# The third of sixteen units moves from the early kind of work to the later kind

## The chip, the cores and the metric

One core of one Trainium2 chip runs one program. The metric is the device time of one execution in microseconds (us). Its engines work in parallel, each through its own queue in order: PE (TensorE, the matrix engine), DVE (VectorE), ACT (ScalarE), POOL (GpSimd) and SP (SyncE, which here issues every transfer). They wait for each other through semaphores. A matrix product leaves its result in PSUM, of which this kernel uses four tiles ("banks" in the code, b_70 to b_73 in its instructions).

## The reference

Windowed attention, half of the heads with a dense window of 32 and half with a dilated one, and behind it a two-layer feed-forward net on the 4,608 tokens (8 batches of 576), 512 features wide and 2,048 inside:

```python
scores = where(mask, q @ k.T / sqrt(D), -1e9)          # 8 batches, 8 heads, 576 tokens, D = 64
attn   = softmax(scores) @ v
x      = attn, heads side by side                      # 4608 x 512
h      = x @ w_in                                      # 512 x 2048
g      = h * tanh(softplus(h))
out    = g @ w_out                                     # 2048 x 512
```

## The kernel before

**Units.** The work is cut into 16 units of 288 tokens (half a batch each), numbered 0 to 15. A unit's attention has two kinds, 0 (dense) and 1 (dilated). Its x goes through the first layer in eight pieces ff*u*.0 to ff*u*.7, each of two groups of twelve 288-column products (every number is held as two f16 parts, and three products of parts are added), and then through the second layer.

**Two kinds of unit.** Units 0, 1 and 2 are early (constants `FIRST = 3` and `DIRECT = 3`). There the masks are added by PE, the probabilities are turned by PE (L684), the values are multiplied in f32 (L710 with tile `vf`), x is turned by PE (L759), and the second layer is plain: sixteen groups of twelve 288-column products (L991, steps fo). Units 3 to 15 are late (`SEVENS = range(3, 16)`). There the masks are added by DVE, the values are held as two stacked f16 parts in `vh` (L551, L553, and three copies by transfer, L559 and L561), the probabilities are split in two by ACT and DVE and turned by a transfer (L671 to L676), and so is x (L750 to L754). Their second layer takes seven products of half size in place of eight (L952, steps fq: 336 products of 144 columns), with sums of parts of the gate made by DVE (L928) and sums of parts of w_out.

**Between the kinds.** Both weights are loaded as raw 64-bit words and split by ACT and DVE (steps wl, wm, ww, ws, wp) in a memory pool named `early`. Step ol gives that pool back and opens `late`, in which the late units' tiles live (among them the raw values `vn`, the turned probabilities `pT`, and one tile `x16` for both kinds' x). When the last plain second layer no longer reads w_out, step rs rescales it in four parts (L847), and steps su make its sums (L866, L859, L862). The late units' seven products need these sums, and the plain second layer must be over before.

**Order.** Nothing is scheduled by a program at build time: the table ORDER lists some 2,000 steps. A step is a generator, and each mention runs it to its next yield, so the table fixes every engine's queue. "=2" behind a name picks the PSUM tile. va is the value product, tx the turning of x, sp the score products, kw and kh products whose results nobody reads.

The lines that the steps below touch most, in transpose_x:

```python
            x16 = take("x16", x16s)[:nq, :4 * nb * P]
            nc.scalar.copy(hi, xs)
            nc.vector.tensor_tensor(lo, xs, hi, op=ALU.subtract)
            nc.sync.dma_start_transpose(x_span(d, kind).rearrange("k (g q) -> k g q", q=nq), x16)
```

ff1 takes the four 128-row blocks of x in the order kind 0, kind 0, kind 1, kind 1, so its third product already needs both kinds.

Of the kernel before, what the change touches and what calls it, by code (L numbers as in the profile page):

```python
# [41 lines left out]
wl0.0.0 mf wl0.3.0 ww0.3.0 wl0.0.1 ld0 ld0 lv0 mf qp0 ww0.0.0 wm0.0.0 ld0 ld0 ww0.0.1 cs1 ww0.0.0 cs0 kw12 lv0  # L42
wl0.3.1 lv1 wm0.3.0 kh30 kw4 wm0.0.1 ww0.0.0 ww0.3.1 ww0.3.0 kw12 ww0.0.1 ld1 sp0.1=0 sp0.1 ww0.0.1 ws0.0=1 lv0
ww0.3.0 wm0.3.0 sp0.0=2 sp0.0 ww0.3.0 sc0.1 ws0.0 sc0.0 sc0.1 ww0.3.0 lv0 ld1 wm0.3.1 sc0.0 ww0.3.1 qp1 ex0.1 ex0.0
ld1 ww0.3.0 ws0.3=3 tp0.1=1 ws0.3 wp0.0.1 tp0.0=0 wp0.3.0 ww0.3.1 sp1.0=2 xa0 wp0.3.0 tp0.1 ld1 sp1.0 wp0.0.0 sc1.0
sp1.1=3 sp1.1 sc1.0 lv0 sc1.1 kw5 sc1.1 wp0.3.1 wp0.0.0 va0.1=1 pr0 tp0.0 pr0 va0.1 ex1.0 va0.1 ex1.1 wp0.3.1 pr0=0
kw3 tp1.1=2 wl0.1.0 va0.0=3 pr0 wl0.2.1 va0.0 va0.1 va0.1 va0.0 tx0.1=0 ww0.1.0 va0.0 wl0.1.1 va0.0 wm0.1.0 wp0.0.1
lv1 fs0.0 tx0.1 tx0.0=1 wl0.2.0 tx0.0 tx0.1 ww0.1.1 lv2 tp1.0=3 ww0.2.1 tx0.0 tp1.1 wm0.1.1 ww0.1.0 ff0.0=0 wm0.2.1
ff0.0 ld2 tp1.0 ld2 wm0.2.0 lv1 ww0.1.0 ff0.7=1 ww0.2.0 ff0.0 ww0.1.1 ww0.2.1 ws0.1=2 ws0.1 ww0.1.1 ff0.6=3 fs0.3
wp0.1.0 ww0.2.0 ff0.7 ww0.2.0 ff0.6 wp0.1.1 ws0.2=2 qp2 ff0.1=0 wp0.1.1 ws0.2 ff0.6 lv1 ff0.7 wl1.0.0 wp0.1.0 fs0.1  # L50
ww0.2.1 fs0.2 lv1 sp2.0=3 wp0.2.0 sp2.0 wp0.2.1 ff0.1 ff0.3=1 ft ff0.1 wp0.2.0 wm1.0.0 ww1.0.0 ff0.3 fs0.4 ff0.2=2
wp0.2.1 sc2.0 ff0.2 ww1.0.0 ww1.0.0 ff0.2 ff0.3 ff0.4=0 gt0.1=0 ff0.4 ff0.4 va1.0=3 va1.1=2 pr1 va1.0 va1.0 ff0.5=1
gt0.3=1 pr1 wl1.0.1 pr1=0 gt0.3 gt0.0=2 ww1.0.1 ld2 ff0.5 pr1 va1.1 va1.0 wm1.0.1 va1.1 ld2 va1.0 wl1.1.0 va1.1
ff0.5 va1.1 sp2.1=0 ww1.0.1 fs1 tx1.0=3 xa1 tx1.0 tx1.1=1 ws1.0=2 tx1.0 wl1.1.1 tx1.1 ww1.1.0 tx1.1 ws1.0 wm1.1.0
sp2.1 sc2.1 gt0.2=3 ff1.2=3 ff1.5=1 wp1.0.0 lv2 ff1.3=2 ld3 ff1.6=0 gt0.0 ff1.2 ww1.0.1 ww1.1.1 ww1.1.0 ff1.5 ff1.2
wp1.0.0 lv2 ww1.1.0 gt0.1 wm1.1.1 ex2.1 wp1.0.1 ff1.6 wl1.3.1 ff1.0=3 ff1.5 lv2 gt0.2 xa2 ff1.3 ww1.1.1 ff1.0
ws1.1=1 wp1.0.1 ff1.3 ff1.7=2 ff1.0 tp2.1=3 ws1.1 wm1.3.1 lv2 ww1.1.1 wp1.1.0 ff1.7 tp2.1 fo0.0.0=1 pr2 fo0.0.1
ex2.0 tp2.0=3 ff1.6 ff1.4=0 wl1.3.0 ff1.4 ff1.7 wp1.1.1 fo0.0.2 pr2 wp1.1.1 pr2=2 wp1.1.0 tp2.0 ff1.1=3 pr2 fo0.0.3
va2.0=2 ww1.3.1 ff1.4 va2.1=0 va2.1 wl1.2.0 fo0.0.3 wm1.3.0 ww1.3.1 va2.0 va2.0 va2.1 va2.0 va2.1 gt1.1=4 ff1.1
ww1.3.0 wl1.2.1 fo0.1.0 gt1.3=5 va2.1 va2.0 tx2.1=0 ww1.3.0 wm1.2.0 gt1.1 tx2.1 tx2.0=2 ld3 tx2.1 tx2.0 fs2 tx2.0  # L60
ww1.3.1 ff1.1 gt1.2=6 ww1.3.0 fo0.1.1 wm1.2.1 ww1.2.1 ww1.2.1 ld3 ws1.3=0 fo0.1.2 qp3 fo0.1.3 ff2.6=2 ww1.2.0
ww1.2.0 fo0.1.3 ff2.0=3 gt1.2 gt1.0=7 ff2.0 ff2.0 gt1.3 ff2.7=1 ff2.2=3 fo0.0.3 gt1.0 fo0.1.3 ws1.3 ww1.2.0 ws1.2=0
wp1.3.1 ww1.2.1 ff2.2 ws1.2 wp1.3.1 wp1.3.0 ld3 wp1.2.1 ff2.6 wp1.2.0 ff2.6 ff2.7 ff2.4=0 ff2.4 ff2.2 sp3.0=2
wp1.2.0 sp3.1=3 sp3.1 ld4 sp3.0 wp1.2.1 ff2.7 wp1.3.0 ff2.4 mr=1 ol ff2.5=0 mr mr ff2.5 fo0.2.0=1 fo0.2.1 sc3.1 lv3
fo0.2.2 fo0.2.3 ld4 ff2.5 ex3.1 fo1.0.0=3 lv3 sc3.0 ex3.0 fo0.2.3 fo1.0.1 lv3 fo0.3.0 gt2.3=2 fo0.3.1 tp3.0 tp3.0
pr3 lv3 pr3 ld4 pr3=0 gt2.2=0 ff2.1=2 tp3.1 tp3.1 pr3 ff2.1 fo0.3.2 tp3.1 pr3 pr3 ff2.3=0 xa4 tp3.1 ld4 ff2.1
gt2.0=3 lv4 fo1.0.2 qp4 fo1.0.3 gt2.0 tp3.0 lv4 vx3 ff2.3 fo1.0.3 fo0.3.3 gt2.3 ff2.3 sp4.1=2 sp4.0=0 sp4.0 lv4 vx3
fo0.2.3 lv4 fo1.0.3 sc4.0 sp4.1 vx3 gt2.1=1 gt2.1 fo1.1.0 fo1.1.1 fo0.3.3 sc4.1 ex4.0 pr4 tp3.0 ld5 gt2.2 qp5
fo1.1.2 fo2.0.0=0 fo1.1.3 ld5 fo1.1.3 fo2.0.1 fo2.2.0=1 va3.0=2 va3.1=3 va3.0 va3.1 pr4 ld5 va3.0 fo2.2.1 va3.0
va3.1 fo0.3.3 pr4=2 tp4.0 tp4.0 pr4 fo2.2.2 fo1.1.3 va3.1 fo2.0.2 pr4 fo1.2.0=2 pr4 ld5 fo2.2.3 fo2.2.3 fo2.0.3  # L70
tp4.0 lv5 sp5.1=3 lv5 xa3 sp5.1 tx3.0 fo1.2.1 lv5 fo1.2.2 lv5 sc5.1 fo2.0.3 ex4.1 fo2.3.0 fo2.3.1 tp4.1 fo2.1.0
tp4.1 sp5.0=3 tp4.1 tx3.0 sp5.0 fo2.1.1 fo2.1.2 fo2.3.2 ld6 vx4 pr5 sc5.0 ex5.1 tx3.0 vx4 tx3.1 tp4.0 fo2.1.3
fo2.0.3 vx4 fo1.2.3 fo2.1.3 fo2.2.3 fo1.2.3 va4.0=3 tp4.1 va4.0 fo1.2.3 fo2.3.3 fo2.1.3 fo1.3.0 fo1.3.1 fo2.3.3
va4.0 tp5.1 tp5.1 fo1.3.2 fo1.3.3 so tx3.1 fo1.3.3 va4.1=0 pr5 tx3.1 rs rs rs fs4 rs va4.1 su0=3 su0 ff3.5=1 ff3.0=2
tp5.1 su0 ff3.0 va4.0 tp5.1 fs3 va4.1 ex5.0 ld6 rs ff3.4=3 tx4.0 su1=1 su0 tx4.0 su1 tx4.0 fo1.3.3 ff3.4 va4.1 ff3.0
ff3.1=2 ff3.4 ff3.1 tp5.0 tp5.0 su0 tx4.1 su1 tx4.1 su1 ff3.5 ff3.7=0 ff3.5 ld6 su0 ff3.2=3 ff3.1 gq3.0.0=0 su0
# [1004 lines left out]
```

## Time and profile before

| | us |
|---|---|
| median of 3 runs | 849.95 (846.66 to 851.33) |
| the profiled execution, its time | 850.15 |
| its span, first to last instruction | 848.4 |
| PE busy in it | 825.8 |

The span is the part that the trace shows; 1.75 us of the profiled execution lie around it. A row of the trace gives a start, a duration, an engine, the line of the kernel, the operation with its output and inputs, and in brackets the idle time ahead of it and who ended it. PE's rows can hold many matmuls merged, with a small overlap at their ends.

### The profile page before, as it was taken

How to read it: one execution, taken by the hardware profiler on the slowest of the kernel's cores; microseconds unless marked ns; L12 is line 12 of the kernel's file. 1: busy time of each engine (PE TensorE's matmuls, PEld its weight loads, DVE VectorE, ACT ScalarE, POOL GpSimd, SP SyncE). 2: the span in 40 equal slices, each digit the busy share in tenths (PEclk: the TensorE clock that was granted, in tenths of full speed). 3: DMA queues.
4: the chain of work that ended last, by engine and by line, in shares of the span. 5: the costliest groups of instructions: out<-in, count | busy, mean ns of one | idle time of the engine just before them, and what ended most of it. 6: DMA issues, size and time to landing. Idle time of an engine off the chain costs nothing.

```text
span 848.4 us, 29902 instructions
## 1 busy us (share of the span) xinstructions
PE 825.8 (97%) x13706; PEld 712.2 (84%) x13706; DVE 600.9 (71%) x770; ACT 489.3 (58%) x608; POOL 40.4 (5%) x80
## 2 busy tenths in 40 slices
...
DMA packets 157581, 98.18 MB, mean 116 GB/s; under 512 B 92496, under 2 KB 150864, under 8 KB 157456
## 3 DMA queue, kind: packets, MB, share of 16 engines
...
q8 instruction: 107, 1.75, 0.9%
...
## 4 chain that ended last, share of the span: by engine, by line
PE 70%; DVE 10%; DMA 9%; SPq 4%; ACT 4%; issue 3%; DVEq 0%; ACTq 0%
PE b L809 33%; PE b L952 25%; PE b L991 5%; PE b L602 3%; PE b L710 2%; DVE g L866 2%; DMA vn<-in_v 1%; DVE g L922 1%; DMA w<-in_w_in 1%; DMA vh<-vh 1%; DMA x<-x 1%; SPq L513 1%; DMA knd<-in_kdT 1%; DVE hm L928 1%; SPq L676 1%
## 5 line engine op out<-in xcount | busy, mean ns | idle before, releaser
L809 PE MATMUL b<-x,w 128*128 128x288 f16 x3072 | 395.2, 286 | 4.3 <-DMA x<-x 2.3
L809 PEld LDWEIGHTS <-w 128*128 128x128 f16 x3072 | 294.3, 97 | 79.1 <-issue 4.3
L922 DVE SCALAR_TENSOR_TENSOR g<-hm,sg,g 128x1152 f16<-128x1152 f32 (+1 forms) x104 | 129.8, 1263 | 70.0 <-ACT g L920 69.8
L815 ACT ACTIVATE hm<-b,fs 128x576 f32<-128x576 f32 x128 | 92.6, 737 | 135.6 <-PE b L809 116.0
L952 PE MATMUL b<-g,w 128*128 128x144 f16 x2496 | 166.6, 226 | 0.6 <-DVE g L922 0.6
L952 PEld LDWEIGHTS <-w 128*128 128x128 f16 x2496 | 159.2, 98 | 3.3 <-issue 0.7
L920 ACT ACTIVATE g<-hm,sg 128x1152 f16<-128x1152 f32 (+1 forms) x104 | 115.7, 1127 | 46.6 <-PE b L952 30.5
L928 DVE TENSOR_TENSOR hm<-hm 128x576 f32<-128x576 f32 x104 | 80.4, 779 | 3.2 <-ACT hm L815 2.2
L966 ACT ACTIVATE y<-b,fo 128x288 f32<-128x288 f32 x52 | 40.4, 780 | 58.7 <-PE b L952 57.3
L991 PE MATMUL b<-g,w 128*128 128x288 f16 x576 | 73.1, 286 | 0.0
L991 PEld LDWEIGHTS <-w 128*128 128x128 f16 x576 | 55.8, 98 | 14.2
L971 DVE SCALAR_TENSOR_TENSOR y<-b,fo,y 128x144 f32<-128x144 f32 x78 | 33.4, 477 | 47.6 <-PE b L952 23.9
L952 PE MATMUL b<-g,g 128*128 128x144 f16 x936 | 66.0, 226 | 0.0
L952 PE MATMUL b<-g,late_sums 128*128 128x144 f16 x936 | 65.4, 226 | 0.0
L952 PEld LDWEIGHTS <-g 128*128 128x128 f16 x936 | 60.8, 98 | 1.4
L952 PEld LDWEIGHTS <-late_sums 128*128 128x128 f16 x936 | 60.2, 98 | 0.5
L618 DVE SCALAR_TENSOR_TENSOR sb<-b,m_p 96x768 f32<-96x768 f32 (+2 forms) x26 | 24.1, 927 | 23.4 <-PE b L602 20.0
L553 DVE SCALAR_TENSOR_TENSOR vh<-vn,s,vh 128x2688 f16<-128x2688 f32 (+1 forms) x13 | 35.2, 2708 | 6.2 <-ACT vh L551 6.2
L551 ACT ACTIVATE vh<-vn,s 128x2688 f16<-128x2688 f32 (+1 forms) x13 | 29.7, 2288 | 11.4 <-issue 7.4
L489 POOL COPY qp<-qn 128x576 f32<-128x576 f32 x15 | 25.0, 1664 | 203.2 <-DMA qn<-in_qT 145.9
L730 DVE TENSOR_TENSOR xs<-b,rec 128x768 f32<-128x768 f32 (+1 forms) x32 | 30.6, 956 | 2.6
L331 DVE TENSOR_REDUCE m<-vn 128x1 bf16<-128x1024 f32 (+1 forms) x19 | 20.3, 1068 | 15.2 <-DMA vn<-in_v 12.7
(131 smaller groups left out, 735.7 us busy)
## 6 DMA issues: line engine op xcount, KB each, us to landing
...
```

The costliest lines, as they stand in the source:

```text
L551: nc.scalar.activation(hi, src, AF.Identity, scale=s)
L553: nc.vector.scalar_tensor_tensor(lo, src, s, hi, ALU.mult, ALU.subtract)
L730: nc.vector.tensor_tensor(xs.rearrange("p (a t h e) -> p a t h e", a=2, h=2, e=D), avv[:, :, :, 1:AW - 1].rearrange("p a t (h e) -> p a t ...
L809: nc.tensor.matmul(ph[:, h, :HT], w1[j][:, c, wi, k * P:(k + 1) * P], x_of(d, xi, c), start=(n == 0), stop=(n == len(seq) - 1))
L815: nc.scalar.activation(d["m"][p][:, half, k0:k0 + 2], ph[:, :, :HT], AF.Mish, scale=d["fs"][:, j:j + 1])
L920: nc.scalar.activation(hi, src, AF.Identity, scale=sg)
L922: nc.vector.scalar_tensor_tensor(lo, src, sg, hi, ALU.mult, ALU.subtract)
L928: nc.vector.tensor_tensor(a, a, b, op=op)
L952: nc.tensor.matmul(acc[e], left(l, e, p, wi)[:, k * P:(k + 1) * P], right(gi, k), start=(n in opens and p == 0 and q == 0), stop=(last and ...
L966: nc.scalar.activation(into(half, t), by(acc), AF.Identity, scale=fo)
L971: nc.vector.scalar_tensor_tensor(o, by(acc)[:, e], fo, o, ALU.mult, ALU.add)
L991: nc.tensor.matmul(po[:, :HT], w2[:, e, j, wi, k * P:(k + 1) * P], d["g"][j][:, gi, k, :], start=(j == 0 and n == 0), stop=(j == NCH - 1 a ...
```

## The change

Three constants go from 3 to 2, so that unit 2 is a late unit: its values are stacked, its probabilities and its x are turned by transfers, its second layer takes seven half-size products, and only units 0 and 1 have a plain second layer. The scale of the output (`fo`) gets a function of its own, since unit 2's scale can be made only behind rs while its other scales are needed ahead of it. The table ORDER is a new one throughout, the start included: kw and kh steps differ, and the loads come in another order.

```diff
-    FIRST = 3
-    DIRECT = 3
-    SEVENS = range(3, 16)
+    FIRST = 2
+    DIRECT = 2
+    SEVENS = range(2, 16)
...
-        if u >= FIRST:
-            nc.scalar.activation(d["fo"], h_o, AF.Identity, scale=d["f_v"])
+        if u > FIRST:
+            out_scale(u)
+
+    def out_scale(u):
+
+        nc.scalar.activation(U[u]["fo"], h_o, AF.Identity, scale=U[u]["f_v"])
...
-             "ex": exps, ... "fs": ff_scales,
+             "ex": exps, ... "fs": ff_scales, "fp": out_scale,
...
-kh30 kw4 wm0.0.1 ww0.0.0 ww0.3.1 ww0.3.0 kw12 ww0.0.1 ld1 sp0.1=0 sp0.1
+kw12 lv1 ww0.3.0 ww0.3.0 ld0 cs0 cs1 xa1 kh162 mf ww0.3.0 ww0.3.0 sp0.0=0
```

What stands where the plain second layers end and the first late unit's first layer begins, on three engines. (Line numbers of the changed kernel are up to 6 higher.)

PE before: the last rows ahead of ff3. pT_2102 with vh is the value product of unit 4, kind 1; x with w_88 is ff3.

```order
L991 MATMUL b_72<-g_102,w_90 128x288
...
L710 MATMUL b_70<-vh,pT_2102 32x65
L809 LDWEIGHTS w_88
L809 MATMUL b_71<-x,w_88 128x288
```

PE after: the last three plain groups, the value product of unit 2, kind 1 (pT_1760), the scores of unit 4 (knp and knd), and ff2 (x with w_86).

```order
L997 MATMUL b_73<-g_101,w_90 128x288
...
L997 MATMUL b_73<-g_104,w_90 128x288
...
L997 MATMUL b_70<-g_97,w_90 128x288
...
L712 MATMUL b_73<-vh,pT_1760 32x65
L604 MATMUL b_71<-knp,qp 32x64 x24
L604 MATMUL b_72<-knd,qn 32x56 x32
L604 MATMUL b_71<-knp,qp 32x64 x12
L604 MATMUL b_72<-knd,qn 32x56 x16
L815 LDWEIGHTS w_86
L815 MATMUL b_70<-x,w_86 128x288
```

Ahead of ff the plain groups and the values of the unit after next stood on PE; now the values of the very unit that ff takes stand there, with four rows of scores between.

DVE before: xs is a unit's normalised x before turning, x_2104 its split into x16. The rows are of unit 3, whose ff comes next; L847 is the rescaling.

```order
L752 TENSOR_TENSOR x_2104<-xs_2817,x_2104 128x768
L997 TENSOR_SCALAR fo<-h_o,f 128x1
L530 TENSOR_REDUCE m_3087<-vn 128x1
L838 TENSOR_REDUCE const_o<-f_o 128x1
L839 RECIPROCAL const_o<-const_o 128x1
L841 TENSOR_SCALAR const_o<-f_o,const_o 128x4
L842 TENSOR_SCALAR const_o<-const_o,top_92 128x1
L843 COPY h_o<-const_o 128x4
L847 TENSOR_SCALAR w_90<-w_90,const_o 128x4096 x3
```

DVE after: the rows of unit 2. L853 is the rescaling of the last part of w_out, L872 the sums, L555 the split of unit 3's values.

```order
L853 TENSOR_SCALAR w_90<-w_90,const_o 128x4096
L730 RECIPROCAL rec<-den 128x12
L732 TENSOR_TENSOR xs_2609<-b_73,rec 128x768
L754 TENSOR_TENSOR x_1762<-xs_2527,x_1762 96x768
L872 TENSOR_TENSOR g_98<-w_90 128x1024
L872 TENSOR_TENSOR g_98<-g_98,w_90 128x1024
L555 SCALAR_TENSOR_TENSOR vh<-vn,s,vh 128x21x128
L754 TENSOR_TENSOR x_1762<-xs_2609,x_1762 128x768
```

The split of x, which was over before the rescaling began, now stands behind it, and kind 0's (xs_2527) behind kind 1's normalising (xs_2609).

## Rows read from the trace of the kernel before

**Rows 1.** The page's busy times, share of the span, instructions.

```profile
PE 825.8 (97%) x13706; PEld 712.2 (84%) x13706; DVE 600.9 (71%) x770; ACT 489.3 (58%) x608; POOL 40.4 (5%) x80
```

**Rows 2.** Windows: stretch, length, busy PE, PEld, DVE, ACT, POOL; clock, DMA share, GB/s.

```profile
0.00:43.05 43.05, 34.50 (x684) 26.74 (x684) 27.48 (x41) 23.84 (x31) 8.68 (x32) 0.92 0.84 268
43.05:142.50 99.45, 93.71 (x1394) 74.19 (x1395) 79.72 (x112) 77.63 (x92) 4.68 (x3) 1.00 0.47 145
142.50:222.00 79.50, 79.23 (x1258) 63.16 (x1256) 57.06 (x75) 37.84 (x52) 5.77 (x11) 1.00 0.71 159
222.00:264.00 42.00, 41.42 (x410) 34.70 (x409) 41.73 (x53) 26.46 (x37) 1.45 (x2) 1.00 0.17 40
```

**Rows 3.** PE by line and shape: busy us, mean ns of one | idle before.

```profile
L991 PE MATMUL b<-g,w 128*128 128x288 f16 x576 | 73.1, 286 | 0.0
...
L952 PE MATMUL b<-g,w 128*128 128x144 f16 x2496 | 166.6, 226 | 0.6 <-DVE g L922 0.6
...
L952 PE MATMUL b<-g,g 128*128 128x144 f16 x936 | 66.0, 226 | 0.0
L952 PE MATMUL b<-g,late_sums 128*128 128x144 f16 x936 | 65.4, 226 | 0.0
```

**Rows 4.** PE in order of time: unit 2's masks, turned probabilities, values, turned x.

```profile
56.57 0.48 PE L589 MATMUL b<-m_b,ident_p 96*96 96x384 bf16 x2
...
75.26 0.51 PE L582 MATMUL b<-m_b,ident_b 96*128 96x128 bf16 x6
...
98.24 0.82 PE L684 MATMUL b<-ident,sb 128*128 128x128 f32 x6
...
103.31 0.66 PE L684 MATMUL b<-ident,sb 96*128 96x96 f32 x6
...
112.39 1.90 PE L710 MATMUL b<-vf,pp 64*32 64x65 f32 x168
...
117.17 1.32 PE L759 MATMUL b<-ident,xs 128*128 128x128 f32 x12
```

**Rows 5.** PE: unit 4's scores; five plain groups; unit 4's values, two kinds; ff3.

```profile
169.13 0.83 PE L602 MATMUL b<-knd,qn 64*32 64x56 f32 x64
169.77 0.94 PE L602 MATMUL b<-knp,qp 64*32 64x64 f32 x70
...
184.59 7.51 PE L991 MATMUL b<-g,w 128*128 128x288 f16 x60
...
209.28 0.93 PE L710 MATMUL b<-vh,pT 128*32 128x65 f16 x72 [0.27 <-DVE h_o L843]
...
217.60 1.08 PE L710 MATMUL b<-vh,pT 128*32 128x65 f16 x96
218.62 23.69 PE L809 MATMUL b<-x,w 128*128 128x288 f16 x192
```

**Rows 6.** ACT, DVE and SP: unit 3 from values to turned x.

```profile
183.23 0.18 ACT L726 ACTIVATE den<-b 128x12 f32<-128x12 f32 x1 [0.25 <-PE b L710]
...
205.23 0.83 ACT L750 CAST x<-xs 128x768 f16<-128x768 f32 x1 [5.70 <-DMA x<-x]
...
185.69 0.96 DVE L730 TENSOR_TENSOR xs<-b,rec 128x768 f32<-128x768 f32 x1
...
206.10 0.96 DVE L752 TENSOR_TENSOR x<-xs,x 128x768 f16<-128x768 f32 x1 [1.15 <-ACT x L750]
...
200.51 1.34 SPq L754 DMA_TRANSPOSE x<-x  x1
```

**Rows 7.** SP: the last of three copies that stack unit 3's values.

```profile
174.54 0.52 SPq L561 DMA_DIRECT2D vh<-vh  x1
```

**Rows 8.** Windows at the start: columns as in rows 2.

```profile
11.50:13.30 1.80, 0.38 (x6) 0.34 (x6) 1.01 (x1) 1.80 (x5) 0.63 (x1) 1.00 1.08 349
13.30:20.20 6.90, 5.25 (x133) 2.83 (x131) 6.04 (x9) 1.17 (x2) 0.66 (x2) 0.51 1.08 308
20.20:30.00 9.80, 7.77 (x174) 5.08 (x180) 7.56 (x11) 8.55 (x10) 1.20 (x1) 1.00 0.55 142
```

More of the change, by code (lines that the diff above doesn't have):

```diff
@@ L41 @@
 ORDER = """
[L42 to L76, printed above, removed]
```

225 lines of the change are left out of this document (131 added, 94 removed).

## The prediction

> **What bounds the kernel now.** I read the busy times first: PE is busy for 825.8 of 848.4 us, DVE for 71% and ACT for 58% [rows 1]. The windows then show where PE's idle time of 22.6 us lies: 8.55 us before the first layer begins at 43.05, 5.74 us while the weights are split, 0.27 us between 142.5 and 222, 0.58 us between 222 and 264 [rows 2], and the rest far behind. So PE's own work sets the end. An edit that takes work off PE shortens the run by that work, unless it makes PE wait; and every wait of PE counts in full. DVE is the second limit in one place only: from 222 to 264, where the sums of w_out are made, it is busy for 41.73 of 42.00 us, and PE still loses only 0.58 us.
>
> The sum is made against the profiled execution, 850.15 us (span 848.4), which is 0.2 us above the median of 849.95. Any difference below 0.5% (4.2 us) cannot be told from no change.
>
> **PE's work: less by 5.1 us.** Unit 2's masks leave PE (0.48 + 0.51), so do the turned probabilities (0.82 + 0.66) and the turned x (1.32); its values cost 1.90 as f32 and 0.93 + 1.08 as stacked f16, as unit 4 shows [rows 4, 5]. That is 0.99 + 1.48 + 1.32 - 0.11 = 3.68 us. The second layer: three plain ones take 73.1 us, 24.37 each; thirteen of seven products take 166.6 + 66.0 + 65.4 = 298.0 us, 22.92 each [rows 3]. That saves 1.45 us, little for one product in eight, because 4,368 products of 144 columns take 68.2 ns each. Scores are the same work. Together 5.1 us, all of it on the path.
>
> The rows thus put a half-size product at 68.2 ns [rows 3]. The Trainium skill, "TensorE: Matmul & The Clock Gate", section "Back-to-back issue gap", speaks against the change here: it gives about 81 ns per product at 128 columns as the sustained pace of weight load and product in turn. By that, 336 products would be an estimated 27.2 us, more than the plain layer's 24.37, PE's saving would fall from 5.1 to 0.8 us, and the forecast below would be 865.3. The trace does not agree: its products are wider and still faster, and the measured pace decides.
>
> **The place where the kinds meet: 12 us lost.** Before, PE goes straight from the plain groups and unit 4's values (217.60) into ff3 (218.62), without a wait [rows 5], because unit 3's x had been turned while two plain second layers were still to do. The order after has no such cover. Behind unit 2's own kind-1 values only unit 4's scores stand on PE, then ff2, whose third product needs both kinds of unit 2's x. Count from the start of unit 2's kind-0 values on PE:
> PE: values 0.93, three plain groups of 7.37 / 5 = 1.47 each, values 1.08, so 6.4; scores of 0.83 + 0.94, so PE has nothing left at 8.2 [rows 5].
> The rest: ACT's denominator (0.18) and DVE's normalising of kind 1 (0.96 and a reciprocal, 1.2 together) bring us to 7.9. Only then does DVE split kind 0's x (0.96), as the order shows, so 8.9. Its transfer took 4.72 us in unit 3, from issue at 200.51 to ACT's start at 205.23, which waited for it because x16 is one tile [rows 6]: 13.6. ACT's copy and DVE's split of kind 1, 205.23 to 207.06, are 1.83: 15.5. A second transfer of 4.7: 20.2. In the 5.6 us between the two splits DVE has two sums and unit 3's values to do, which just fit.
> So PE waits 20.2 - 8.2 = 12 us. If the transfers land in 3.3 us it is 9; if unit 3's values delay the second split, 15. What waits behind it is everything: PE's queue is in order, and ff2 stands ahead of all later work. Nothing of the loss comes back, because PE has no idle time behind it to give up.
>
> **The clock: 2.5 us.** Where PE had been busy for only 0.38 of 1.80 us, its granted clock then stood at 0.51 from 13.3 to 20.2, the 1.2 GHz level, although PE was soon busy again [rows 8]. A wait of 12 us is longer. PE was working again for some 5 us of that low stretch, at half pace, so I take 2.5 us; ends 0 and 3.5 (the whole 6.9 us).
>
> **The stretch of the weights and the start: 1 us more.** From 43.05 to 142.5 PE did 93.7 us of work, DVE 79.7, ACT 77.6 [rows 2]. In the new order PE has there 5.7 us less of unit 2's attention, ten groups of ff2 less (14.7) and two plain groups and a unit's scores less (4.7): 68.6. DVE loses eight operations of about 0.96 [rows 6], two maxima and three gate operations, some 13 us, and keeps 67. PE's lead over DVE is almost gone. If PE stays busy for 94% of the stretch, its idle time falls from 5.7 to 4.3; if DVE stays busy for only 80%, the stretch lasts 84 us and PE's idle rises to 15. At the start, 162 short kh products stand in place of the mixed kw and kh products, and may spare the low clock of rows 8 (up to 2.6 us), though the first layer waits there for DVE. Ends: 4 us gained and 9.5 lost; I take 1 us lost, nearer to PE's row, since part of DVE's idle time was spent on PE.
>
> **What hangs on the pool's release.** Unit 2's values need `vn` loaded, `vh` split and copied three times. In unit 3 the last copy was issued at 174.54, 32 us behind the end of the weights at 142.5 [rows 2, 7]. After the masks of step mr the new order has 23 plain groups (33.9) and two kinds of scores on PE before unit 2's values. So this just fits; I price it at nothing, and at 3 us if it does not.
>
> **The sums of w_out: 0.5 us.** DVE begins them earlier against ff2 than it did against ff3, by the length of the wait, but now the attention of units 3 and 4 falls into the same stretch. PE lost 0.58 us there [rows 2, 3]. Ends 0 and 6; I take 0.5 more.
>
> **Sum.** 850.15 - 5.1 + 12.0 + 2.5 + 1.0 + 0.5 = 861.05, so 861.
>
> **Rivals.**
> Not slower, by the front. DVE and ACT get rid of unit 2's early work before the weights are split, PE no longer falls into the low clock, and the first 142.5 us shrink by more than the sum above loses. For it: 8.55 + 5.74 us of idle time stand there, and 2.6 us of half clock. Against it: PE's lead over DVE shrinks too. It decides from 12 + 2.5 + 0.5 - 5.1 = 9.9 us gained ahead of the release. With 10 us it gives 850, with 14 it gives 846. Chance 0.13, of which 0.05 is faster.
> The wait is covered. PE reaches unit 2's values later than the chain needs, or ff2 finds x turned: 850.15 - 5.1 = 845. For it: nothing in the rows; the order shows no work that could cover. It would take another reading of who waits for what. Chance 0.07.
> DVE becomes the bound. The sums, two units' attention and the gates of unit 2 meet from ff2 on, and PE waits for the first gates and for unit 3's x: 6 us more than the forecast, 867. For it: 41.73 of 42 us busy. Against it: DVE starts on the sums while PE waits. Chance 0.12.
> That the change does not do what it says: the half-size layer's saving cannot fail on 4,368 measured products, and it is only 1.45 us.
>
> **Chances and range.** The forecast's own case, a wait of 9 to 15 us with a net loss, has 0.68. It is slower in nearly all of its range: 853 to 866. With the rivals: faster 0.12, within 0.5% 0.10, slower 0.78. The range of 8 in 10 reaches from 849, which takes in the front's gain up to 10 us, to 870, which takes in DVE's case; 845 and below is left out.
>
> **What would show it.** A single idle stretch of PE of 9 to 15 us ahead of the first L815 rows of unit 2, ended by the turned x (transfer of x); the granted clock at one half for some microseconds behind it; PE's busy time lower by 5 us, apart from products at low clock and more kh and kw products at the start; the masks of step mr on PE at 115 to 125 in place of 142; fourteen half-size layers at 22.9 us each. I am wrong if PE goes into ff2 without a wait, or if the first 142 us shrink by far more than the work moved out of them.

## The result, and the profile after

The changed kernel takes 860.75 us (median of 4 runs, 860.31 to 862.05); the kernel before, on the same chip, 850.64 us (4 runs). The ratio is 1.0125, with a 95% interval from 1.0095 to 1.0154: slower by 10.1 us. The forecast was 861. The profiled execution took 860.31 us, its span is 858.5 us, so the spans differ by 858.5 - 848.4 = 10.1 us as well.

The page's busy times, against [rows 1]:

```profile
PE 829.1 (97%) x13958; PEld 722.1 (84%) x13962; DVE 619.2 (72%) x788; ACT 497.5 (58%) x616; POOL 36.9 (4%) x82
```

Windows of the kernel after: stretch, length, busy PE, PEld, DVE, ACT, POOL, granted clock, DMA share, GB/s. The first two rows answer to the first two of [rows 2]; the third is the place where the kinds meet, the last two are ff2 and what follows, with the sums of w_out.

```profile
0.00:52.16 52.16, 40.31 (x813) 34.25 (x815) 28.44 (x41) 24.78 (x33) 10.66 (x31) 0.90 0.73 234
52.16:122.50 70.34, 69.18 (x894) 55.06 (x890) 63.01 (x90) 60.14 (x70) 1.36 (x1) 1.00 0.50 159
167.30:178.10 10.80, 0.96 (x9) 0.43 (x8) 10.18 (x9) 4.61 (x6) 1.47 (x2) 0.68 0.85 167
178.10:222.00 43.90, 42.05 (x674) 33.43 (x674) 43.31 (x52) 27.88 (x39) 0.25 (x2) 0.96 0.67 143
222.00:264.00 42.00, 41.59 (x640) 36.64 (x638) 38.85 (x51) 27.52 (x36) 1.81 (x4) 1.00 0.45 102
```

PE is idle for 9.84 of the 10.80 us of the third row. But look at DVE in it and behind it: 10.18 of 10.80, then 43.31 of 43.90. That column is what the prediction read too lightly. The first row says something else that was not forecast: the first layer begins at 52.16, 9.1 us later than before, of which 5.8 us are PE's busy time (40.31 against 34.50).

PE in order of time, from the values of unit 2 (L712) to ff2 (L815); in brackets the idle time ahead and who ended it:

```profile
159.03 0.94 PE L712 MATMUL b<-vh,pT 128*32 128x65 f16 x72
159.90 4.58 PE L997 MATMUL b<-g,w 128*128 128x288 f16 x36
164.42 1.08 PE L712 MATMUL b<-vh,pT 128*32 128x65 f16 x96
...
166.85 0.44 PE L604 MATMUL b<-knd,qn 64*32 64x56 f32 x23
169.04 0.29 PE L604 MATMUL b<-knd,qn 64*32 64x56 f32 x6 [1.75 <-issue]
172.90 0.66 PE L815 MATMUL b<-x,w 128*128 128x288 f16 x2 [3.56 <-DMA x<-x]
178.10 10.36 PE L815 MATMUL b<-x,w 128*128 128x288 f16 x70 [4.54 <-DMA x<-x]
...
203.88 3.11 PE L815 MATMUL b<-x,w 128*128 128x288 f16 x24 [1.17 <-DVE xs L732]
...
207.72 3.17 PE L958 MATMUL b<-g,w 128*128 128x144 f16 x48
```

The chain is the one that the prediction walked through: PE out of work at 167.28, 8.25 us behind the first value product (8.2 forecast), and PE goes on with the second transfer of x at 178.10, 19.07 us behind it (20.2 forecast). The idle time comes in three pieces, 1.75 + 3.56 + 4.54 us, with few products between them. The first piece, inside the scores, is put to issue: the engine waited for nothing that the profile shows. Behind the wait the granted clock is about one half for some 4 us:

```profile
178.10:180.00 1.90, 1.90 (x9) 1.19 (x9) 1.90 (x4) 1.25 (x3) 0.00 (x0) 0.50 0.95 174
180.00:182.00 2.00, 2.00 (x12) 1.37 (x11) 2.00 (x3) 0.06 (x1) 0.00 (x0) 0.64 1.01 282
```

The second layers, by shape, against [rows 3]:

```profile
L958 PE MATMUL b<-g,w 128*128 128x144 f16 x2688 | 179.9, 226 | 0.3 <-DVE g L928 0.3
L958 PE MATMUL b<-g,g 128*128 128x144 f16 x1008 | 71.1, 226 | 0.0
L958 PE MATMUL b<-g,late_sums 128*128 128x144 f16 x1008 | 70.8, 226 | 0.0
L997 PE MATMUL b<-g,w 128*128 128x288 f16 x384 | 48.8, 286 | 0.0
```

Fourteen half-size layers take 321.8 us, 22.99 each, and the plain ones 24.4 each.

### The profile page after: what moved, and what is told of

Read it like the earlier page. It is cut to its first block, busy times and chain, and to the rows that moved or that the text cites. A ratio compares the mean times of both kernels' runs of the same rounds, so it can differ in the third digit from the quotient of the medians.

```text
span 858.5 us, 30492 instructions
## 1 busy us (share of the span) xinstructions
PE 829.1 (97%) x13958; PEld 722.1 (84%) x13962; DVE 619.2 (72%) x788; ACT 497.5 (58%) x616; POOL 36.9 (4%) x82
## 4 chain that ended last, share of the span: by engine, by line
PE 84%; DVE 6%; issue 3%; DMA 3%; ACT 2%; SPq 1%; POOL 1%; POOLq 0%; DVEq 0%; ACTq 0%
PE b L815 39%; PE b L958 33%; PE b L997 6%; PE b L604 3%; PE b L712 3%; DVE g L928 1%; DMA w<-in_w_in 1%; DMA vh<-vh 1%; DVE g L872 1%; DMA x<-x 1%; DMA vf<-in_vd 1%; ACT hm L821 1%; DVE hm L934 1%; PE b L1024 0%; DVE xs L732 0%
## 5 line engine op out<-in xcount | busy, mean ns | idle before, releaser
L815 PE MATMUL b<-x,w 128*128 128x288 f16 x3072 | 399.0, 286 | 11.3 <-DMA x<-x 8.1
L815 PEld LDWEIGHTS <-w 128*128 128x128 f16 x3072 | 295.0, 98 | 86.4 <-issue 7.6
L958 PE MATMUL b<-g,w 128*128 128x144 f16 x2688 | 179.9, 226 | 0.3 <-DVE g L928 0.3
L958 PEld LDWEIGHTS <-w 128*128 128x128 f16 x2688 | 171.8, 98 | 4.0 <-issue 0.5
L928 DVE SCALAR_TENSOR_TENSOR g<-hm,sg,g 128x1152 f16<-128x1152 f32 (+1 forms) x112 | 140.8, 1271 | 45.8 <-ACT g L926 45.7
L926 ACT ACTIVATE g<-hm,sg 128x1152 f16<-128x1152 f32 (+1 forms) x112 | 125.0, 1127 | 60.8 <-PE b L958 35.5
L934 DVE TENSOR_TENSOR hm<-hm 128x576 f32<-128x576 f32 x112 | 86.2, 772 | 4.7 <-ACT hm L821 2.8
L958 PE MATMUL b<-g,g 128*128 128x144 f16 x1008 | 71.1, 226 | 0.0
L958 PE MATMUL b<-g,late_sums 128*128 128x144 f16 x1008 | 70.8, 226 | 0.0
L958 PEld LDWEIGHTS <-g 128*128 128x128 f16 x1008 | 65.5, 98 | 1.6
L958 PEld LDWEIGHTS <-late_sums 128*128 128x128 f16 x1008 | 65.0, 98 | 0.7
L997 PE MATMUL b<-g,w 128*128 128x288 f16 x384 | 48.8, 286 | 0.0
L997 PEld LDWEIGHTS <-w 128*128 128x128 f16 x384 | 37.0, 98 | 9.5
L555 DVE SCALAR_TENSOR_TENSOR vh<-vn,s,vh 128x2048 f16<-128x2048 f32 (+1 forms) x14 | 37.5, 2682 | 5.4 <-ACT vh L553 5.4
L553 ACT ACTIVATE vh<-vn,s 128x2048 f16<-128x2048 f32 (+1 forms) x14 | 31.7, 2262 | 4.4 <-issue 2.1
L620 DVE SCALAR_TENSOR_TENSOR sb<-b,m_p 96x768 f32<-96x768 f32 (+2 forms) x28 | 25.9, 925 | 10.8 <-PE b L604 10.4
L732 DVE TENSOR_TENSOR xs<-b,rec 128x768 f32<-128x768 f32 (+1 forms) x32 | 30.6, 956 | 3.4 <-PE b L958 0.5
L754 DVE TENSOR_TENSOR x<-xs,x 96x768 f16<-96x768 f32 (+1 forms) x28 | 26.6, 949 | 8.4 <-ACT x L752 8.4
```

The lines of the kernel that those rows point to most:

```text
L553: nc.scalar.activation(hi, src, AF.Identity, scale=s)
L555: nc.vector.scalar_tensor_tensor(lo, src, s, hi, ALU.mult, ALU.subtract)
L732: nc.vector.tensor_tensor(xs.rearrange("p (a t h e) -> p a t h e", a=2, h=2, e=D), avv[:, :, :, 1:AW - 1].rearrange("p a t (h e) -> p a t ...
L815: nc.tensor.matmul(ph[:, h, :HT], w1[j][:, c, wi, k * P:(k + 1) * P], x_of(d, xi, c), start=(n == 0), stop=(n == len(seq) - 1))
L926: nc.scalar.activation(hi, src, AF.Identity, scale=sg)
L928: nc.vector.scalar_tensor_tensor(lo, src, sg, hi, ALU.mult, ALU.subtract)
```

## The experiments

All are made from the kernel after, except the last. To compare them without the start, which differs between executions (unit 2's values begin anywhere from 157.72 to 160.46 us), I use two lengths of each profiled execution: **A**, from the first value product of unit 2 (159.03 in the kernel after) to the first product of its second layer (207.72), and **B**, from there to the end of the span. Each A and B is of one execution. Edits far ahead of this stretch alone move A by 0.3 us (48.43 and 48.36 in the two runs on the start), so a difference of 0.3 us in A says nothing.

| kernel | median, us | A | DVE busy in A | clock in A | B |
|---|---|---|---|---|---|
| after | 860.75 | 48.69 | 45.75 | 0.89 | 650.78 |
| weights' steps later | 859.29 | 48.43 | 46.11 | 0.89 | 651.35 |
| unit 2's x by PE | 860.92 | 49.03 | 46.25 | 0.93 | 651.28 |
| values and split earlier | 869.00 | 56.85 | 53.80 | 0.82 | 650.68 |
| 12 additions left out | 859.97 | 48.42 | 37.77 | 0.86 | 649.41 |
| both of these: x by PE, 12 left out | 856.72 | 44.37 | 38.23 | 0.92 | 650.67 |
| x by PE, another order on DVE | 867.10 | 52.59 | 45.08 | 0.94 | 652.82 |
| x by PE, ten additions on POOL | 867.57 | 52.98 | 47.87 | 0.90 | 653.68 |
| 160 products in the wait | 871.65 | 48.84 | 46.46 | 1.00 | 663.28 |
| 80 products in the wait | 890.37 | 49.98 | 46.38 | 0.93 | 680.53 |
| 128 products in the wait | 862.03 | 48.44 | 46.53 | 1.00 | 651.59 |

### The start

What holds up the start in the kernel after: ACT waits for raw weights (L380) with unit 0's last probabilities (L689) behind it, and PE waits for those.

```profile
38.31 1.12 ACT L380 ACTIVATE w<-w 128x1024 f32<-128x1024 f32 x1 [4.75 <-DMA w<-in_w_in]
...
40.32 0.79 ACT L689 COPY pp<-b 128x768 f32<-128x768 f32 x1
```

```profile
41.16 4.25 PE L1024 MATMUL b<-ones 128*128 128x96 f32 x20 [5.21 <-ACT pp L689]
```

The first experiment moves these steps of the weights behind unit 0's attention.

```diff
-sc1.0 wm0.1.0 pr0 ld1 ww0.1.0 tp0.1 ... va0.0=3 wm0.1.1 pr0 lv1 va0.1 va0.0 ww0.1.0 va0.1
+sc1.0 pr0 ld1 tp0.1 ... va0.0=3 pr0 lv1 va0.1 va0.0 va0.1
...
-tx0.0 sp1.1 sc1.1 ww0.1.1 tp1.0 ff0.0=1
+tx0.0 sp1.1 sc1.1 wm0.1.0 ww0.1.0 wm0.1.1 ww0.1.0 ww0.1.1 tp1.0 ff0.0=1
```

> The kernel after, with four steps of the weights (wm0.1.0, the first two of ww0.1.0, wm0.1.1: ACT's two conversions and what follows them) moved behind unit 0's attention in the table; the work is the same. In the kernel after, ACT waits 4.75 us for a transfer of raw weights with unit 0's last probabilities behind it in its queue, and PE has 4.25 us of work in 5.21 us of idle time around 41 us. Theory 1 (the late start of the first layer, 52.16 us against 43.05 before, is on the path): the first layer begins about 45 to 48 us and the run takes 854 to 857 us. Rival (the weights are ready no earlier, and PE waits for them later instead): the first layer begins earlier but PE's idle time up to the end of the weights grows by as much, and the run stays at 860 to 862 us.

Measured: 859.29 us, 1.5 us less than after. The wait for `pp` is gone and the first layer begins at 48.41, 3.75 us earlier; unit 2's values come only 1.31 us earlier (157.72). PE in this kernel:

```profile
48.41 1.78 PE L815 MATMUL b<-x,w 128*128 128x288 f16 x12
...
53.32 0.61 PE L392 MATMUL b<-w,ones 128*128 128x512 bf16 x2 [1.62 <-DVE w L423]
```

Neither range held. The wait was real, but its larger part came back: the moved weights were now late themselves, and PE waits 1.62 us for them. About a third of the earlier start reached unit 2's values. The gain of 1.5 us is small against the spread: the two intervals overlap (a ratio of 1.0063 to 1.0123 here, 1.0095 to 1.0154 for the kernel after). The start itself, in this kernel:

```profile
0.00:48.41 48.41, 41.65 (x813) 35.59 (x816) 27.70 (x40) 21.78 (x30) 10.94 (x31) 0.86 0.74 240
```

PE is idle for 6.76 us of it, less than the 8.55 us of the kernel before; what is left of the late start is busy time, 41.65 against 34.50 us.

The second asks whether DVE's work sets the stretch of the weights. It leaves out DVE's third step on each word of w_out.

```diff
-            nc.vector.scalar_tensor_tensor(lo[:, c], hi[:, c], -0x80000000, a[:, c], ALU.bitwise_and, ALU.bitwise_or)
+            if k == 0:
+                nc.vector.scalar_tensor_tensor(lo[:, c], hi[:, c], -0x80000000, a[:, c], ALU.bitwise_and, ALU.bitwise_or)
...
-        x, dst, s = lo.bitcast(F32), w_dst(k, g, p), ready[k, g]
+        x, dst, s = (hi if k else lo).bitcast(F32), w_dst(k, g, p), ready[k, g]
```

> The kernel after with eight operations of DVE (1.17 us each, 9.4 us) of the splitting of w_out left out, all between 80 and 117 us; the words that are split there are the raw high words, so the weights are others. Start and everything behind the weights are unchanged. It asks what sets the stretch of the weights, in which PE was busy for 69.18 of 70.34 us, DVE for 63.01. Theory (PE's own work sets it, as the busy share says): PE's masks of step mr still come at 122 to 122.5 us, the run stays at 860 to 861.5 us. Rival (DVE's queue sets it, PE's small waits being only where it shows): the masks come at 118 to 120 us, and the run takes 857 to 858.5 us.

Measured: 860.89 us, no change, as the theory had it. The stretch, beside the second window row of the kernel after:

```profile
52.00:122.50 70.50, 69.34 (x931) 55.16 (x918) 54.18 (x83) 60.05 (x70) 2.13 (x1) 1.00 0.51 164
```

DVE has 9 us less to do, PE's 69.34 stay. Once the first layer runs, PE's own work sets this stretch, the side to which the prediction leaned.

### The wait ahead of ff2

Unit 2's x is turned by PE, as in the early units, so that no transfer stands in the chain.

```diff
-        if not d["direct"]:
+        if not d["direct"] and u != 2:
...
-sp4.1=2 tx2.0 sp4.0 ... su1=1 tx2.1 pr3
+sp4.1=2 tx2.0=0 sp4.0 ... su1=1 tx2.1=3 pr3
```

> The kernel after, with unit 2's x alone turned by PE again (twelve f32 products, then ACT's and DVE's split out of PSUM), no transfer, same places in the table. Theory 1 (PE's 9.84 us of waiting is the two transfers in a row and the single x16 tile): the wait falls to 2.5 to 4 us, PE has 1.3 us more work, and the run takes 853.5 to 856 us, since the low clock goes too. Rival (DVE's queue, the rescaling and the sums ahead of the splits, sets it): the wait stays above 7 us, and the run is at 859 to 861 us.

Measured: 860.92 us. PE in this kernel:

```profile
170.57 0.38 PE L604 MATMUL b<-knd,qn 64*32 64x56 f32 x18 [1.04 <-issue]
172.99 1.37 PE L815 MATMUL b<-x,w 128*128 128x288 f16 x6 [1.69 <-ACT x L765]
176.94 9.52 PE L815 MATMUL b<-x,w 128*128 128x288 f16 x64 [2.58 <-DVE x L767]
187.79 0.55 PE L712 MATMUL b<-vh,pT 128*32 128x65 f16 x36 [1.33 <-issue]
192.47 3.10 PE L815 MATMUL b<-x,w 128*128 128x288 f16 x24 [0.70 <-ACT hm L821]
197.58 1.63 PE L815 MATMUL b<-x,w 128*128 128x288 f16 x12 [0.31 <-DVE xs L732]
...
204.89 3.11 PE L815 MATMUL b<-x,w 128*128 128x288 f16 x24 [1.61 <-DVE xs L732]
```

The waits for the transfers, 8.1 us, became waits of 4.3 us for the split. Further waits came a little later, the longest for unit 3's normalised x (xs), which frees the PSUM tile that ff2 needs next. In all, PE's idle time in A fell from 11.23 to 9.33 us, and its busy time rose by 2.2 us (37.46 to 39.70), for PE now turns x itself. Stretch A did not shrink at all. So my theory, that the chain of transfers sets the end, was wrong or only half of it; with the work that this edit adds to PE, the run alone does not say which.

The second attempt changes the order alone: both value products together ahead of the last plain groups, the first split ahead of the rescaling.

```diff
-va2.0=1 va2.0 tp3.0 tp3.0 fo1.3.2 fo1.3.3 va2.0 fo0.3.3 ... va2.1=3 rs rs rs rs
+va2.0=1 va2.0 pr3 va2.1=2 va2.1 tp3.0 tp3.0 va2.0 va2.1 va2.0 xa2 tx2.0 tx2.0 tx2.0 va2.1 fo1.3.2 fo1.3.3 fo0.3.3 ... rs rs rs rs
```

> The kernel after, with order alone changed: both kinds of unit 2's values stand together ahead of the last three plain groups, and kind 0's x is normalised, split and sent off ahead of the rescaling of w_out; kind 1's x still has to wait for the one x16 tile. Theory 1 (the wait is a chain of fixed length that begins with the values): the chain begins for kind 1 some 4 us earlier, the wait falls from 9.84 to 6.5 to 7.5 us, and the run takes 857.5 to 859 us. Rival (the earlier work of DVE delays the rescaling and the sums by as much, and PE pays it in ff2): the wait falls but the run stays at 860 to 862 us.

Measured: 869.00 us, 8.3 us worse. DVE's first normalising in this kernel, and PE:

```profile
160.29 0.22 DVE L730 RECIPROCAL rec<-den 96x12 f32<-96x12 f32 x1 [6.25 <-ACT den L728]
```

```profile
170.28 1.16 PE L604 MATMUL b<-knd,qn 64*32 64x56 f32 x60 [4.08 <-DVE p L675]
...
178.90 5.03 PE L815 MATMUL b<-x,w 128*128 128x288 f16 x22 [5.99 <-DMA x<-x]
...
195.15 0.85 PE L712 MATMUL b<-vh,pT 128*32 128x65 f16 x36 [5.00 <-DVE sb L620]
```

My edit put the rescaling behind the normalising, so DVE had nothing to do for 6.25 us and then 53.80 us of work in stretch A in place of 45.75. Kind 0's transfer was issued earlier (163.45, 167.97 in the kernel after), but kind 1's split now stands behind three parts of the rescaling, and its transfer was issued no earlier (175.44, 174.78 in the kernel after). So the wait ahead of ff2 did not fall, and this run says nothing on theory 1. The loss comes behind it: PE waits 5.00 us more for DVE's step on unit 4's masks (L620), and its mean clock in A is 0.82. Stretch A is longer by 8.16 us, DVE's work in it by 8.05: what the edit pushed into DVE's queue there was paid in full. The rival had the direction, not the size.

This gave the next theory, two limits of equal length side by side, and two runs to test it: twelve of the twenty additions for the sums of w_out are left out, once alone, once with x turned by PE.

```diff
         tt(pair(a11, 0), pair(a21, 0), sub)
-        tt(t, pair(a11, 1), add)
         yield
-        tt(t, pair(a21, 1), sub)
         yield
...
```

> The kernel after without 12 of the 20 additions of 1.22 us that DVE makes for the sums of w_out (8 or 9 of them stand ahead of 204 us, some 10 us of DVE); the parts that they would add are left out of the sums, all else and every place in the table stays, and unit 2's x is still turned by two transfers. So far: with the x turned by PE the wait ahead of ff2 fell from 9.84 to some 4 us and the run did not get shorter, and DVE is idle for only 0.86 us from 160.6 to 236 us. Theory 2 (two limits of equal length stand side by side in 160 to 204 us, the chain of the transfers and DVE's queue): with DVE's load alone taken away the chain still holds PE for 8 to 10 us, only the waits at 189 and 204 us go, and the run takes 857.5 to 860 us. Theory 1 (the chain of transfers alone): within 0.7 us of 860.75. Theory 3 (DVE's queue alone, the transfers wait for nothing but DVE): the wait falls by most of the 10 us, 850 to 853 us.

> Both at once: the kernel after without the same 12 additions (those parts are left out of the sums) and with unit 2's x turned by PE. Theory 2 (two limits side by side): only now does PE run through; its wait ahead of ff2 is 2 to 4 us, the later waits go, PE has 1.3 us more work, and the run takes 851.5 to 854.5 us, far below both edits alone. Theory 1 (the chain alone): the same as with the x turned by PE alone, 860 to 861 us. Theory 3 (DVE alone): the same as without the additions alone.

Measured: 859.97 us for the first, 856.72 us for both (ratio to before 1.0079, 1.0053 to 1.0104). Stretch A, in a window of the first and then of the second kernel:

```profile
160.07:208.49 48.42, 38.31 (x799) 28.92 (x798) 37.77 (x49) 28.71 (x40) 3.36 (x7) 0.86 0.62 134
```

```profile
160.46:204.83 44.37, 39.96 (x811) 30.15 (x810) 38.23 (x49) 28.49 (x40) 3.37 (x7) 0.92 0.67 129
```

Taking 8 us of DVE's work away shortens A by 0.3 us, taking the transfers away alone does not shorten it (0.3 us longer), both together shorten it by 4.3. The medians say the same: 860.75, 859.97, 860.92 and 856.72 us, and every run of the last is below every run of the others. That is the form of two limits side by side, and neither of the one-limit theories fits the pair; the first run alone is only 0.1 us outside what theory 1 allowed. The gain of the pair was 2 to 5 us short of the forecast: PE still waits for ACT's and DVE's copies of x (1.38 and 1.30 us) and 1.35 us for issue, and its clock is at 0.92.

If DVE's queue is the second limit up to the first product of the second layer, a better order on it should help, with no work left out.

```diff
-xa2 tx2.0=0 ... rs va2.1 tx2.0 tx2.0 tp3.1 pr3 su0 su1=1 tx2.1=3 pr3 tp4.1 sp4.1 ld5 tx2.1 su1 tx2.1 sc4.0
+xa2 tx2.0=0 tp3.1 sp4.0=1 tx2.0 su0 sp4.1=2 tx2.0 sp4.0 rs va2.1 sp4.1 tx2.1=3 tp3.1 tx2.1 su0 tx2.1 pr3 su1=1 pr3 tp4.1 ld5 su1 sc4.0
...
-va3.1=3 ex4.1 su0 va3.1 ga2.0 ff2.2 va3.1 pr4 fo0.3.3 va3.1
+va3.1=3 ex4.1 va3.1 ff2.2 va3.1 va3.1 su0 su0 ga2.0 pr4 fo0.3.3
```

> The kernel with unit 2's x turned by PE, nothing left out, and DVE's queue in another order: both splits of unit 2's x stand right behind the normalising, ahead of four additions and the split of unit 3's values, and unit 3's normalised x (which frees the PSUM tiles that PE waits for at 197 and 204 us) stands ahead of sums and maxima. DVE's work is the same, some 7 us of sums stand later. In the kernel with x by PE alone PE waited 1.69 + 2.58 + 0.70 + 0.31 + 1.61 = 6.9 us at these places. Theory 2 (DVE's queue is the second limit, and what PE waits for is its order up to 204 us): from PE's first value product of unit 2 to its first product of the second layer 43 to 45 us in place of 49.0, and a run of 855 to 857 us. Rival (DVE's total work decides, the sums that stand later are waited for just as long behind it): the first product earlier, but waits of 3 us or more between 208 and 260 us, and a run of 859 to 861 us.

Measured: 867.10 us, 6.2 us worse than x by PE alone. PE and DVE in this kernel:

```profile
172.65 3.11 PE L815 MATMUL b<-x,w 128*128 128x288 f16 x22 [0.64 <-ACT x L765]
181.91 8.69 PE L815 MATMUL b<-x,w 128*128 128x288 f16 x48 [6.15 <-DVE sb L620]
```

```profile
167.51 0.76 DVE L767 TENSOR_TENSOR x<-b,x 128x576 f16<-128x576 f32 x1 [2.66 <-ACT x L765]
...
172.63 0.96 DVE L767 TENSOR_TENSOR x<-b,x 128x768 f16<-128x768 f32 x1 [2.04 <-ACT x L765]
```

PE now has all of x at 172.65, 5.4 us earlier than in the kernel after, and does two groups; then it waits 6.15 us for a PSUM tile, which DVE frees by its step on unit 4's masks (L620). That step stands behind the same sums as before, and behind 2.66 + 2.04 us in which DVE, with the splits at the head of its queue, waits for ACT's copies. DVE's idle time in A rose by 4.7 us (49.03 - 46.25 = 2.78, now 52.59 - 45.08 = 7.51), A by 3.6. Neither side of the expectation held: no gain, and the loss lies ahead of the first product, not behind it. What it shows is again that what DVE loses in this stretch, the run loses for the most part.

Ten of the additions on POOL, which does next to nothing there:

```diff
-        eng = nc.gpsimd if SUMS_BY_POOL else nc.vector
+        eng = nc.gpsimd if e == 1 else nc.vector
```

> The kernel after with unit 2's x turned by PE, and with the ten additions of one half of the sums (su1) on POOL in place of DVE, nothing left out. POOL is busy for 0.25 us from 178 to 222 us. Theory 2 (DVE's queue is the other limit): DVE loses 12 us of work, 8 of them ahead of 204 us, and if POOL makes one addition in less than 2.5 us the run takes 853 to 857 us. Rival (DVE waits for POOL's slower additions at L868, in its own queue, or its own operations slow down beside POOL's): 860 us or more.

Measured: 867.57 us. The rival held, by its second branch. DVE's split of unit 3's values and one addition, and POOL's additions beside them:

```profile
169.41 4.97 DVE L555 SCALAR_TENSOR_TENSOR vh<-vn,s,vh 128x2688 f16<-128x2688 f32 x1 [1.68 <-ACT vh L553]
...
187.31 3.15 DVE L872 TENSOR_TENSOR g<-g,w 128x1024 f32<-128x1024 f32 x1
```

```profile
166.91 2.13 POOL L872 TENSOR_TENSOR g<-g,w 128x1024 f32<-128x1024 f32 x1
...
199.37 4.18 POOL L872 TENSOR_TENSOR g<-g,w 128x1024 f32<-128x1024 f32 x1
```

An addition takes POOL 2.13 us where DVE is idle for most of it (busy for 0.76 us from 166.91 to 169.04), and up to 4.18; DVE's split takes 4.97 in place of 3.02 us, its addition 3.15 in place of 1.22. Not every pair collides: beside DVE's two maxima at 192.61 (2.33 us, as without POOL) POOL's addition keeps its 2.13 us.

### The low clock, and what the inserted products did

Short products fill PE's wait, so that its clock does not fall. This was run with 160, 80 and 128 of them.

```diff
-ex4.0 ff2.1=0
+ex4.0 kh160 ff2.1=0
```

> The kernel after, with 160 short products whose result nobody reads (about 0.057 us each, some 9 us) on PE in place of most of the idle time ahead of ff2. Nothing else moves, and x is still turned by two transfers one after the other. Theory 1 (the half clock behind the wait is caused by the wait and costs about 1.6 us): the clock stays at 1.0 behind 178 us and the run takes 859 us. Rival (the low clock costs nothing, because DVE's sums limit that stretch anyway): within 0.4 us of 860.75. If the products run past the landing of x, up to 861.5.

> The kernel after with 80 short products ahead of ff2 in place of 160. With 160, PE reached the first product of unit 2's second layer 48.8 us behind the first value product, as in the kernel after (48.7), and then took 663.3 us to the end in place of 650.8, with waits that the trace puts to issue (3.2 us at 309 us, in the middle of a run of products). Theory (the inserted instructions shift where PE's instruction stream has to be loaded, and it is by chance which loads meet busy transfers): 48.5 to 49 us as before for the first part, and a second part of 651 to 664 us that does not go with the count. Rival (the 160 products changed something else, such as the clock or the PSUM tile): half the loss, a second part of 657 us. If the low clock behind the wait is on the path, the first part is shorter by 0.8 us or more.

> The kernel after with 128 short products ahead of ff2, which are 256 instructions of PE (a weight load and a product each). From the first product of unit 2's second layer to the end the kernel after takes 650.8 us; with 160 such products (320 instructions) ahead it took 663.3, with 80 (160 instructions) 680.5, and the waits were put to issue, inside runs of narrow products. The page shows instructions being loaded in packets of 16.4 KB. Theory (PE's instruction stream is loaded in pieces, and where a piece ends among the work decides; that a piece is 256 instructions is an assumption of this run): 128 products shift everything by one whole piece, so the second part is back at 650 to 652 us, the first part stays at 48.5 to 49.3 us, and the run takes 860 to 861.5 us. Rival (the inserted products do harm in another way, growing or falling with their number): 660 us or more for the second part, 870 us or more for the run.

Measured: 871.65, 890.37 and 862.03 us. With 128, the two windows that answer to the third and fourth of the kernel after:

```profile
167.30:178.10 10.80, 7.03 (x141) 6.64 (x141) 10.43 (x10) 4.25 (x6) 1.55 (x2) 1.00 0.86 175
178.10:222.00 43.90, 40.65 (x681) 32.80 (x680) 43.31 (x52) 27.66 (x39) 0.26 (x2) 1.00 0.68 146
```

The clock is 1.00 throughout (0.68 and 0.96 without the products), and the third product of ff2 starts at 177.54, as early as before relative to the values. Yet stretch A is 48.44 us, 0.25 less, and PE's busy time from 178.10 on falls by 1.40 us without any gain: PE waits that much longer in ff2.

```profile
187.46 0.55 PE L712 MATMUL b<-vh,pT 128*32 128x65 f16 x36 [1.18 <-ACT hm L821]
...
203.27 3.11 PE L815 MATMUL b<-x,w 128*128 128x288 f16 x24 [1.61 <-DVE xs L732]
```

In the kernel after, these two places cost 0.21 us (ACT) and 1.17 us (DVE). The last wait of the stretch ends with DVE's normalising in both kernels. So the half clock costs some 1.6 us of PE's work (an estimate: 1.90 us at 0.50 and 2.00 us at 0.64) and next to nothing of the run.

What the 160 and 80 products cost lies for the most part elsewhere, in stretch B, 12.5 and 29.7 us, up to hundreds of us behind the edit (with 80, A is 1.3 us longer as well). Neither of the first two expectations had such a size. Rows of PE with 160, and then the longest waits with 80 (line, who was waited for, us in total, times, longest):

```profile
309.18 0.42 PE L815 MATMUL b<-x,w 128*128 128x288 f16 x2
312.82 1.46 PE L815 MATMUL b<-x,w 128*128 128x288 f16 x6 [3.22 <-issue]
```

```profile
PE b L604 <- issue: 12.6, 7, 3.1
PE b L712 <- issue: 12.6, 9, 2.1
```

These waits stand inside runs of products that have no reason to wait. With 80 they are in scores and values (L604, L712), 23.2 us of them in stretch B; with 160 they are in the wider products that follow scores or values (8.0 us in L815 and L958). Scores are where PE runs through its instructions fastest: 96 of them take 1.16 us ahead of the wait at 312.82, some 12 ns each, where a product of ff takes some 123 ns [rows 5]. The page of the kernel after has a row for instructions among its DMA queues (packets, MB, share):

```profile
q8 instruction: 109, 1.79, 0.9%
```

That is 16.4 KB in a packet. The last run put the reading to the test: 128 products are 256 instructions, and if the stream comes in pieces of 256, they shift it by a whole piece. Stretch B went back to 651.59 us, within the theory's range; the run, 862.03 us, is 0.5 above it. It is one count, and it fits pieces of 256; other counts with the same remainder were not run. The Trainium skill, "Runtime: NRT & Kernel Launch", section "Instruction fetch mechanics", says the same of the pieces, 16 KiB or 256 instructions each, and that crossing from one to the next is mostly hidden. The first agrees with these runs; the second holds for the kernel after (B has no wait for issue that the timeline shows) and fails with 80 products, where 23.2 us of stretch B are waits for issue.

### DVE's room in the kernel before

If one plain layer less is one cover less for DVE, the kernel before should have room for more work on DVE.

```diff
+            for _ in range(5 if u == 4 else 1):
                 amax(m[:, 0:1], src[:, :n0])
             yield
+            for _ in range(5 if u == 4 else 1):
                 amax(m[:, 1:2], src[:, n0:])
```

> The kernel before with eight more operations of DVE (the two maxima of unit 4's values of 1.21 us, each five times in place of once: 9.7 us more), nothing left out; they stand at 178 to 192 us, under the plain second layers, where DVE was busy for 12 of 20 us. Theory (in the kernel before, the plain groups on PE hide DVE's work ahead of ff3, so DVE has time there that costs nothing, and the change takes one such layer, 24.4 us of cover, away): within 0.8 us of the time before, and PE without a wait ahead of ff3. Rival (DVE is a second limit in the kernel before as well): 3 to 9 us longer.

Measured: 860.05 us (858.72 to 862.84; ratio 1.0100, 1.0059 to 1.0141): 9.9 us longer for 9.7 us of work. The rival had the direction, and the loss is above its 3 to 9 us; my theory is refuted for this place. PE in this kernel:

```profile
189.45 1.76 PE L712 MATMUL b<-vh,pT 128*32 128x65 f16 x132 [4.63 <-ACT y L1006]
195.94 0.19 PE L338 MATMUL b<-m,ones 128*128 128x2 bf16 x1 [2.59 <-DVE xs L732]
```

In the kernel before, DVE was idle for 8 us from 180 to 200, but most of the idle time lay behind its normalising of unit 3 (xs, L732) and not ahead of it. The added maxima stand ahead of it. The first five hold up a scale of the output (DVE, 188.34) that ACT's step y needs, the second five hold up xs, and PE waits for 4.63 + 2.59 us. It then falls to a clock of 0.92 from 178 to 222 (1.00 before), so 7.2 us of the loss are waits and most of the rest is slower products: the five plain groups behind them take 9.05 us in place of 7.51 [rows 5]. An idle share is no room. That the same work placed behind xs would have cost nothing was not tried. (Some 3 us of this profiled execution, which took 862.84 us, were lost ahead of 150 us, where the edit has no part.)

## Why the prediction was right, and where it was not

The forecast of 861.0 us stands against 860.75. Its terms against the two traces:

| term | forecast | measured, us |
|---|---|---|
| PE's work | -5.1 | the other rows leave -5.1 of the 10.1 for it; second layers -1.4 of the -1.45; PE's busy time 3.3 more in all, of which 10.2 are products that nobody reads (22.9 against 12.7 us), so without them 6.9 less, in which stretches at half clock differ too |
| wait where the kinds meet | +12 | +9.84 |
| clock | +2.5 | +1.6 of PE's work (estimate), at most 0.25 of the run |
| weights and start | +1 | +5.3 |
| release of the pool | 0 | 0: no wait ahead of the values at 159.03 |
| sums of w_out and all behind | +0.5 | -1.5: +1.7 to 264 us, -3.2 behind it |

**The wait.** Its two ends, 8.25 and 19.07 us, were forecast at 8.2 and 20.2, step by step and in the right order. The second transfer was the term that was off: issued at 174.78, it was in use at 178.10, 3.3 us, where [rows 6] gave 4.7; the first took 4.96.

**Weights and start.** This step failed by 4 us. The stretch from the first layer to the masks of step mr became 28.91 us shorter (99.25, for the masks stood at 142.30 before, to 70.34). By the prediction's count 25.1 of it is the work that moved out, so it gained 3.8, where 94% would have given 1.4: PE stayed busy for 98% of it. The start lost 9.1 where I looked for a gain from the short products, and its clock is no higher than before (0.90 against 0.92). The order does show ACT's two steps on the weights ahead of `pp`; I did not ask when their transfer would be issued. The run with these steps moved accounts for 3.75 of the 9.1 us of the first layer's delay and for 1.5 us of the run. The other 5.4 us are PE's busy time, as its window shows: products that nobody reads take 23.1 us in it, 12.7 before. Whether PE would only wait in their place was not tried.

**Behind the place.** The -1.5 is PE's idle time from there on, 6.5 us against 8.1 before. It does not come from the sums: from 178.10 to 264 PE is idle for 2.3 us, where the stretch of the sums before has 0.58 [rows 2], so this term was 1.7 and not 0.5. The gain lies behind 264 us, 4.3 us of idle time in place of 7.5: waits of the kernel before for transfers of x (2.3 us) and of turned probabilities (1.1 us) are not there in the kernel after. The prediction had no term for that, and why they are gone was not tried.

The total is right because a loss of 4.3 us more at the start and a loss of 2.2 + 0.9 + 2.0 us less at and behind the wait nearly cancel. That they do is luck.

**What was wrong in the reasoning** is the sentence on which the sum rests, that every wait of PE counts in full. From 159 to 208 us two limits of nearly the same length stand side by side: the chain of values, normalising, split and transfers, and DVE's queue, which is busy for 45.75 of 48.69 us. Shown by the runs, in stretch A: the waits for the transfers removed, no gain, though PE's own work there rose by 2.2 us with it; the half clock removed, 0.25 us; 8 us of DVE's work removed, 0.3 us; the first and the third together, 4.3 us. The other way round, what delays DVE there is paid in full or for the most part (8.05 us of work and 8.16 of A; 4.7 us of idle time and 3.6 of A). The prediction's "in one place only" was too narrow for the kernel before as well, where 9.7 us of work on DVE from 180 on cost 9.9. The prediction's rival that DVE becomes the bound had put 6 us on top of the forecast; in truth DVE's limit lies under the wait and hardly adds to it. Had the chain been 5 us shorter, the forecast would have fallen with it, to 856, where the run with x turned by PE stayed at 860.92.

That the rows could have told: the order put a unit's normalising, two splits, two sums and unit 3's split of values into those 20 us, and I had written that they "just fit". An engine that just fits was a second limit here.

Of what the prediction named as signs, nearly all came: an idle stretch of 9 to 15 us ended by the transfer of x, though in three pieces and not a single one, the clock at one half behind it (0.50 from 178.1 to 180, 0.64 to 182), the masks of step mr at 122.51, and half-size layers of 22.99 us. PE's busy time without the products that nobody reads fell by 6.9 us, where 5 were named. With the half-size layers, 4,704 products of 144 columns at 68.4 ns, the Trainium skill's pace of about 81 ns at 128 columns ("TensorE: Matmul & The Clock Gate", section "Back-to-back issue gap") is refuted for this kernel once more.

No version here beats the kernel before. The best one that computes everything is the one with the weights' steps moved, 859.29 us.
